# Five weight chunks ahead of U and V, block products in another order, and a last pair of heads with narrow matmuls in most slots

## The chip, the cores and the metric

One NeuronCore of one Trainium2 chip. The metric is device time in microseconds (us) of one execution, without the host; lower is better. Engines are named as in the profile: PE (matrix multiplies), PEld (its weight loads, which overlap), DVE, ACT, POOL, and SP, which issues the DMAs. Each engine takes its instructions in the order in which the program has them.

## What is computed

Three stages on a batch of 2 with 768 positions (reference, cut to what matters):

```python
# 1 attention: q, k, v [2, 8, 768, 64], masked by clusters of heads' queries and keys
mask = q_assign[:, :, :, None] == k_assign[:, :, None, :]
scores = np.where(mask, scale * np.matmul(q, k.transpose(0, 1, 3, 2)), -1e9)
attn = np.exp(scores - np.max(scores, axis=-1, keepdims=True))
x = np.matmul(attn / (np.sum(attn, axis=-1, keepdims=True) + 1e-09), v)   # -> [2, 768, 512]
# 2 mixer over positions and channels
theta = x @ w_theta
y = einsum(w_tok_r, x * np.cos(theta)) + einsum(w_tok_i, x * np.sin(theta))
u = x + y
x = u + np.maximum(u @ w_ch, 0.0)
# 3 low-rank mixer, then a wide layer: U [768, 32], V [32, 768], w_ch1 [512, 2048], w_ch2 [2048, 512]
u = x + (x.transpose(0, 2, 1) @ U @ V).transpose(0, 2, 1)
out = u + np.maximum(u @ w_ch1, 0.0) @ w_ch2
```

## The kernel before

x is kept transposed, as eight tiles `xT` of 128 channels by 768 positions (four of them, t = 0 to 3, per batch b; `hf` is a half of 384 positions). The program is written out by hand in the order in which each engine runs it, so an instruction waits for every earlier one on its engine as well as for its own inputs. PE has eight PSUM banks in a ring. Products in near-fp32 precision are made of three passes, with each factor split in a high and a low part: `wh`, `xh`, `uh`, `gh` and `wl`, `xl`, `ul`, `gl`.

**Weights** arrive as 64-bit words and are converted on the chip, one chunk (`Convert`) after the other in the order of a queue: ACT L385 (`magnitude`), then three DVE operations, L389 (`bits`), L393 (`top`), L397 (`low`), then ACT L402 makes `wh` and POOL L406 `wl`. A chunk is 128x768, or 128x512 where it is one of w_ch1. Each call of `conv_step()` that the program makes at fixed places issues the next DVE operation of the front chunk, and behind the last of them the two splits when the next step comes; `conv_until(dst, i)` steps on until a chunk is there. Three staging buffers hold loaded chunks. U and V are chunks too: from U the ACT L615 makes four block-diagonal tiles `ub` in 16 copies, from V ACT L621 and DVE L626 make `vs`. `weigh_pair(k)` takes two chunks of w_ch1 together and makes the sums of blocks of which the last stage's products are formed (ACT L465 and L478, POOL L466 to L480).

**Attention** goes by eight pairs of heads, g = 0 to 7, each in six slots p. A slot makes scores (`st`, PE L303, full 128-column matmuls) for which ACT L308 takes the exponentials `p`; from those come `pv` (L316) and the sums `l` (L335), in matmuls of 32 columns, "narrow" below. A unit of `next_pv` is eight narrow matmuls in the trace's count. Before, units stand only in the slots of `BURST = (2, 5)`, six in each, and `sum_keys` (24 narrow `l`) beside them; `max_rows` (L281 to L284) in slot 2 makes the row maxima `mrow`, which ACT L284 copies into `qp` for the second half of the pair's scores. `fill` issues what stands in the list `bg`, or conversion steps, up to a budget per slot. In the last pair (g = 7, `not nxt`) `bg` gets the splits of four finished tiles, `split_x` (ACT L510 `xh`, POOL L512 `xl`), at a cost of 0, so that all of them go in one call of `fill`.

**Mixer and low rank.** Theta and the position mixing (L525 to L574) are followed by `chmix(b, e)` (L585, L590: the product with w_ch; four per batch). `turn` (DVE L601) transposes finished tiles into `xt`. `low1(b)` is x@U, 24 matmuls of `xt` with `ub` (L636, 48 in the trace's count), `low2` the product with `vs`. The program has chmix(0, 0 to 3), each with `conv_step(3)` or `conv_step(2)`, then steps until U and V are there, chmix(1, 0), low1(0), chmix(1, 1), low2, chmix(1, 2 and 3).

**The wide layer, plain part:** four blocks f of w_ch1 by three pieces c of the positions. `ff1(c, f)` (L708) gives `g`, ACT L713 and DVE L715 split it into `gh` and `gl` (three buffers each), and `ff2(c, f)` (L727) adds its product with w_ch2 into four accumulators, two blocks behind (`AHEAD`). w2 chunk 1 covers rows up to f = 2, chunk 2 is first needed by ff2(0, 3). Beside them run DVE sums of halves (`u_sum`, L676) and their splits (`split_sum`, ACT L682, POOL L683: `u0t`, `u1t`).

**The wide layer, block products:** for k = 2 to 7 and both batches a `Quartet` makes four quarter results from seven products (`step`, six matmuls of L754 each) with DVE sums (L762), and `keep` turns each result into `g` by two ACT operations (L766, L767) and POOL L768. Its eight units (`unit`, six matmuls of L806 each) stand between the steps of the next quartet; unit 0 needs `g[1, 0]` and `g[0, 0]`. The temporaries of the sums (`temp`) take turns in the buffers of `gh` and `gl`. Between the steps of the first quartet stand the last two ff2, behind its steps 1 and 3.

```python
conv_load.extend(ff[:6])            # chunks ahead of U and V
conv_load.append(Convert(u_in, S, 0, [lambda c, g=g: keep_u(c, g) for g in range(4)], 32, 4))
conv_load.append(Convert(v_in, S, 0, [keep_v, keep_vl], 32))
conv_load.extend(ff[6:])
```

Before, the queue behind the three chunks of w_ch is (w1 is w_ch1, w2 is w_ch2): w1 0, w1 1, w2 0, w1 2, w1 3, w2 1, U, V, w2 2, then the pairs of w1 for the block products with a chunk of w2 now and then.

Of the kernel before, what the change touches and what calls it, by code (L numbers as in the profile page):

```python
# [41 lines left out]
def tile_cluster_block(ctx: ExitStack, tc: tile.TileContext, qk, v, cent, wth, wr, wi, wch,  # L42
                       u_in, v_in, w1, w2, cst, out):
    nc = tc.nc
# [408 lines left out]
    w1_t, w1p_t, lower = {}, {}, {}  # L453
# [242 lines left out]
    GF = 4  # L696
# [45 lines left out]
    class Quartet:  # L742
# [26 lines left out]
            self.g[i, hf] = t  # L769

        def step(self, n):
            x, y = (("11", "11"), ("12", "21"), ("s2", "t2"), ("s3", "t3"), ("s1", "t1"), ("22", "t4"), ("s4", "22"))[n]
            ps = bank("q")
            self.products(ps, x, y)
            if n == 0:
                self.u1 = self.temp(0)
                nc.scalar.activation(out=self.u1, in_=ps[:, :HALF], func=AF.Copy)
            elif n == 1:
                r = self.temp(1)
                self.add(r, ps, self.u1)  # L780
                self.keep(0, 0, r)
            elif n == 2:
                self.add(self.u1, ps, self.u1)
            elif n == 3:
                self.u2 = self.temp(0)
                self.add(self.u2, ps, self.u1)
            elif n == 4:
                r = self.temp(1)
                self.add(r, ps, self.u2)
                self.add(self.u1, ps, self.u1)  # L790
                self.keep(1, 1, r)
            elif n == 5:
                self.add(self.u2, ps, self.u2)
                self.keep(1, 0, self.u2)
            else:
                self.add(self.u1, ps, self.u1)
                self.keep(0, 1, self.u1)
# [41 lines left out]
    def attention():  # L839


        ORDER = [(0, 0), (0, 2), (0, 4), (1, 0), (1, 2), (1, 4)]
        BURST = (2, 5)
        pvq = deque()
        held[0] = True

        def next_pv():
            g, kt, hf = pvq.popleft()
            pv(g, kt, hf)
            if kt == NT - 1 and hf:  # L850
                pv_out(g)

        for g in range(NG):
            nxt = g + 1 < NG
            if nxt:
                load_v(g + 1)
            if g + 2 < NG:
                bg.extend(split_items(g + 2, nc.gpsimd))
                bg.extend(assign.pop(g + 2))
            if g + 3 < NG:  # L860
                for i in range(2):
                    load_raw(g + 3, i)
            if g == 1:
                conv_load.extend(weigh_in(wth, NP * DM, wth_t))
                conv_start()
            if g == 2:
                tok = [c for p in zip(weigh_in(wr, NT * S, wr_t), weigh_in(wi, NT * S, wi_t)) for c in p]
                conv_load.extend(tok[:6])
                conv_start()
                late = tok[6:]  # L870
            if g == 6:
                conv_load.extend(late)
                conv_start()
            if not nxt:
                for t in range(NP):
                    bg.append((0, lambda t=t: split_x(0, t, nc.gpsimd)))
            order = [(1, 0), None, (1, 2), None, (1, 4), None] if g == 0 else ORDER
            for p in range(NT):
                ready = len(pvq)
                if order[p]:  # L880
                    h, a = order[p]
                    scores_pair(g, h, a)
                    if h:
                        pvq.extend((g, kt, hf) for kt in (a, a + 1) for hf in range(2))
                if g == 0 and p < 2:
                    mask_direct(1, p, nc.scalar if p else nc.vector)
                if nxt:
                    max_pair(g + 1, p // 3, 2 * p % 6)
                    if p % 3 == 2:
                        max_join(g + 1, p // 3)  # L890

                while conv_after:
                    conv_after.popleft()()
                if p == 3 and g + 2 < NG:
                    mask_rows(g + 2)
                if g > 0 and p == 5:
                    bg.appendleft((.95, lambda: norm_x(g - 1)))
                    bg.appendleft((.97, lambda: spread(g - 1)))
                fill(2. if not nxt else 4.8 if p in BURST else .3)
                if p in BURST:  # L900
                    if p == 2 and g > 0:
                        max_rows(g, 1)
                        sum_keys(g - 1, 1)
                    if p == 5:
                        if nxt:
                            max_rows(g + 1, 0)
                        sum_keys(g, 0)
                    for _ in range(min(ready, 6)):
                        next_pv()
                    if p == 5 and g + 3 < NG:  # L910
                        (_, sims), *assign[g + 3] = assign_items(g + 3)
                        sims()
                if g > 0 and p == 2:
                    row_sums(g - 1)
            while bg:
                fill(.5)
        held[0] = False
        while len(pvq) > 1:
            next_pv()
        nc.scalar.activation(out=warm, in_=warm, func=AF.Sin)  # L920
        next_pv()
        sum_keys(NG - 1, 1)
# [95 lines left out]
    def mixer():  # L1018
# [5 lines left out]
        for n in range(len(seq) + LEAD):  # L1024
# [21 lines left out]
            if n == 11:  # L1046
                conv_load.extend(weigh_in(wch, NP * DM, wch_t))
                c2 = weigh_in(w2, NF * DM, w2_t)
                ff = []
                for k in range(NQ):  # L1050
                    if k == 1:
                        later = ff.pop()
                    if k < GF // 2:
                        ff.extend(Convert(w1, NF * DM, 2 * k + j, keep_split(w1p_t), width=DM) for j in range(2))
                    else:
                        ff.extend(weigh_pair(k))
                    if k == 1:
                        ff.append(later)
                    while c2 and c2[0].c0 < (k + 1) * 2 * DM:
                        ff.append(c2.pop(0))  # L1060
                conv_load.extend(ff[:6])
                conv_load.append(Convert(u_in, S, 0, [lambda c, g=g: keep_u(c, g) for g in range(4)], 32, 4))
                conv_load.append(Convert(v_in, S, 0, [keep_v, keep_vl], 32))
                conv_load.extend(ff[6:])
                conv_start()
            if 20 <= n <= 23:
                clear_u(n - 20)
# [29 lines left out]
        for n, w in enumerate(fs):  # L1097
            ff1(*w)
            if n == 0:
                low1(1)  # L1100
            if n in (1, 2):
                low2(1, 2 * n - 2)
                low2(1, 2 * n - 1)
# [12 lines left out]
        for k in range(GF // 2, NQ):  # L1116
            for b in range(2):
                q = Quartet(k, b)
                for n in range(7):
                    q.step(n)  # L1120
                    if was:
                        was.unit(n)
                    elif n in (1, 3):
                        ff2(*fs[(n - 1) // 2 - AHEAD])
                    if 0 < n < 6:
                        conv_step()
                if was:
# [62 lines left out]
```

## Time and profile before

| what | value |
|---|---|
| median of 3 runs | 697.5 us (696.27 to 698.05) |
| the profiled execution | 697.62 us |
| its span, from the first to the last instruction | 695.8 us |
| mean granted clock of PE, of full speed | 0.99 |
| PE busy | 672.8 us (97%) |
| DVE, ACT, POOL busy | 508.6, 348.4, 280.4 us |

The profile is that of one execution, whose span lies inside its time. Times in its rows are from the span's start. A row gives the start, the time from the first start to the last end of a group of like instructions, the engine, the line, what is written from what, and how many; in square brackets stand the idle time of the engine before it and what ended it. Matmuls overlap each other, so a stretch of PE is read from start to start.

### The profile page before, as it was taken

To read this page: it belongs to the slowest core of one execution; us is meant where nothing else is said; L and a number is where in the kernel's file an instruction comes from. 1 tells how busy PE (TensorE), PEld (TensorE's weight loads), DVE (VectorE), ACT (ScalarE), POOL (GpSimd) and SP (SyncE) were. 2 spreads that over 40 slices of the span, in tenths; PEclk is the share of its full clock that TensorE was granted. 3 is DMA by queue.
4 is the path that set the end of the run, shared out by engine and by line. 5 is a ranking of instruction groups with operands and counts; after the bars stand their busy time and mean duration, and the time that the engine had idled before them with its cause. 6 is when DMAs were issued, how large, how long until landed. Compare 5 with 4: busy or idle time off the path is not lost.

```text
span 695.8 us, 11957 instructions
## 1 busy us (share of the span) xinstructions
PE 672.8 (97%) x4563; PEld 576.0 (83%) x4564; DVE 508.6 (73%) x879; ACT 348.4 (50%) x713; POOL 280.4 (40%) x277
## 2 busy tenths in 40 slices
PE   8899999999998999999999969999989999999997
PEld 3567766756755599999999969898889999999997
DVE  6887898898997474468583957679487877877554
ACT  7657657656758444554555152334344444444221
POOL 8422313323227331114244112248655766656321
PEclk9899999999999999999999989999999999999999
DMA  6769788567423210002121130012213122210013
GB/s 208 196 144 264 196 192 243 159 165 190 141 91 106 77 31 3 1 24 85 57 71 24 58 106 1 0 31 75 78 34 90 62 60 90 61 32 1 0 40 143
DMA packets 21833, 63.15 MB, mean 91 GB/s; under 512 B 4272, under 2 KB 7216, under 8 KB 21776
## 3 DMA queue, kind: packets, MB, share of 16 engines
q1 hardware_dynamic: 21776, 62.39, 31.5%
q8 instruction: 36, 0.59, 0.3%
q14 instruction: 21, 0.17, 0.1%
HBM read 40.94 MB, written 3.15 MB: 63 GB/s over the span
## 4 chain that ended last, share of the span: by engine, by line
PE 82%; DVE 6%; ACT 5%; POOL 3%; issue 2%; DMA 2%; SPq 0%; POOLq 0%; DVEq 0%; ACTq 0%
PE y L567 14%; PE acc L806 14%; PE q L754 11%; PE pv L316 9%; PE st L303 7%; PE g L708 5%; PE th L525 5%; PE l L335 4%; PE acc L727 4%; PE smax L251 3%; PE h L585 2%; ACT p L308 2%; DVE mx L255 2%; PE h L636 2%; DMA st<-in_wth_dram 1%
## 5 line engine op out<-in xcount | busy, mean ns | idle before, releaser
L406 POOL TENSOR_TENSOR wl<-cv,wh 128x768 fp32r<-128x768 f32 (+1 forms) x33 | 60.6, 1838 | 109.8 <-ACT wh L402 92.6
L255 DVE TENSOR_REDUCE mx<-smax 128x1 f32<-128x512 f32 x144 | 89.6, 682 | 15.9 <-PE smax L251 15.9
L806 PE MATMUL acc<-g,wh 128*128 128x384 f32 x384 | 98.1, 335 | 2.9 <-POOL g L768 1.8
L308 ACT ACTIVATE p<-st 128x512 f32<-128x512 f32 x192 | 78.9, 513 | 43.2 <-PE st L303 42.2
L567 PE MATMUL y<-wh,z 128*128 128x384 f32 x384 | 87.6, 340 | 0.3 <-ACT z L545 0.3
L768 POOL TENSOR_TENSOR g<-sum,g 128x384 fp32r<-128x384 f32 x48 | 53.7, 1121 | 81.6 <-ACT g L767 74.2
L762 DVE TENSOR_TENSOR xT<-acc,xT 128x384 f32<-128x384 f32 x96 | 53.1, 555 | 37.4 <-PE acc L806 37.0
L303 PE MATMUL st<-qp,kp 128*128 128x256 f32 (+1 forms) x384 | 78.7, 349 | 0.3 <-ACT qp L284 0.2
L303 PEld LDWEIGHTS st<-qp,kp 128*128 128x128 f32 x384 | 58.7, 192 | 17.3 <-issue 5.3
L806 PEld LDWEIGHTS acc<-g,wh 128*128 128x128 f32 x384 | 69.3, 188 | 3.8 <-POOL g L768 2.4
L567 PEld LDWEIGHTS y<-wh,z 128*128 128x128 f32 x384 | 66.9, 188 | 0.5 <-ACT z L545 0.5
L766 ACT ACTIVATE sum<-sum 128x384 f32<-128x384 f32 x48 | 25.1, 524 | 81.7 <-DVE sum L762 81.7
L316 PE MATMUL pv<-p,v 128*32 128x384 f32 x768 | 65.5, 486 | 0.0
L806 PE MATMUL acc<-g,wl 128*128 128x384 f32 x192 | 64.1, 334 | 0.0
L762 DVE TENSOR_TENSOR sum<-q,sum 128x384 f32<-128x384 f32 x84 | 45.4, 552 | 19.3 <-PE q L754 16.9
L551 POOL TENSOR_TENSOR z<-tht,z 128x256 fp32r<-128x256 f32 x24 | 20.0, 834 | 92.9 <-ACT z L545 92.8
L316 PEld LDWEIGHTS pv<-p,v 128*32 128x32 f32 x768 | 31.6, 110 | 30.1 <-issue 21.6
L393 DVE SCALAR_TENSOR_TENSOR cv<-st,cv 128x768 int32<-128x768 int32 (+2 forms) x47 | 50.3, 1071 | 0.7
L397 DVE SCALAR_TENSOR_TENSOR cv<-st,cv 128x768 int32<-128x768 int32 (+2 forms) x47 | 48.8, 1038 | 0.5
L567 PE MATMUL y<-wl,z 128*128 128x384 f32 x192 | 48.8, 335 | 0.0
L251 PE MATMUL smax<-kp,qp 128*128 128x512 f32 x192 | 44.0, 348 | 3.0 <-ACT qp L177 1.9
L251 PEld LDWEIGHTS smax<-kp,qp 128*128 128x128 f32 x192 | 32.9, 191 | 12.7 <-issue 2.9
(171 smaller groups left out, 1508.8 us busy)
## 6 DMA issues: line engine op xcount, KB each, us to landing
st<-in_w_dram SPq DMA_DIRECT2D x17, 512.0 KB, 3.6
st<-in_w_dram SPq DMA_DIRECT2D x10, 768.0 KB, 4.2
raw<-in_qk_dram SPq DMA_DIRECT2D x16, 384.0 KB, 4.9
qp<-hi SPq DMA_DIRECT2D x26, 192.0 KB, 2.9
st<-in_wr_dram SPq DMA_DIRECT2D x6, 768.0 KB, 4.4
st<-in_wi_dram SPq DMA_DIRECT2D x6, 768.0 KB, 4.4
kp<-hi SPq DMA_DIRECT2D x32, 96.0 KB, 3.0
qp<-lo SPq DMA_DIRECT2D x32, 96.0 KB, 2.7
```

What stands on the lines that cost most here:

```text
L251: nc.tensor.matmul(out=ps[:, c:c + w], lhsT=qp[s, h, 0][:, (a + j) * P:(a + j + 1) * P], rhs=kp[s, h, 0][:, k0:k0 + w], start=True, stop=True)
L255: nc.vector.tensor_reduce(mx_t[g, h][:, o:o + n], ps.rearrange("p (n w) -> p n w", n=n), axis=AX.X, op=ALU.max)
L303: nc.tensor.matmul(out=ps[:, c:c + n], lhsT=kp[s, h, w][:, (a + j) * P:(a + j + 1) * P], rhs=qp[s, h, w][:, q0:q0 + n], start=(w == 0), st ...
L308: nc.scalar.activation(out=pt[g, h, a + j][:, q0:q0 + n], in_=ps[:, c:c + n], func=AF.Exp, scale=float(D) ** -0.5)
L316: nc.tensor.matmul(out=pvt[g][hf][r:r + 32, :HALF], lhsT=v_t[g][:, kt, r:r + 32], rhs=pt[g, r // 64, kt][:, cols(hf)], start=(kt == 0), st ...
L393: nc.vector.scalar_tensor_tensor(t, self.hw, SIGN, t, op0=ALU.bitwise_and, op1=ALU.bitwise_or)
L406: nc.gpsimd.tensor_tensor(t[:, :c.w], c.t, f32(c.hi[:, :c.w]), op=ALU.subtract)
L567: nc.tensor.matmul(out=yps[u, j][hf][:, :HALF], lhsT=lhs, rhs=w[st][e][:, hf * HALF:(hf + 1) * HALF], start=(st == 0 and n == 0), stop=(st ...
L754: nc.tensor.matmul(out=ps[:, :HALF], lhsT=w[a][:, j * P:(j + 1) * P], rhs=u_block(self.b, y, e, j), start=(n == 0), stop=(n == 5))
L762: nc.vector.tensor_tensor(out, ps[:, :HALF], x, op=ALU.add)
L768: nc.gpsimd.tensor_tensor(t[:, 1], r, f32(t[:, 0]), op=ALU.subtract)
L806: nc.tensor.matmul(out=ps[:, :HALF], lhsT=wv[a], rhs=self.g[i, hf][:, x], start=(m == 0), stop=(m == 5))
```

## The change

Three things are edited. First, in the last pair of heads the splits cost 1 in `bg`, `sum_keys(6, 1)` goes from slot 2 to slot 0, `sum_keys(7, 0)` stays in slot 5, and the units of `pv` stand as 2, 2, 2, 0, 4, 4 in the six slots instead of 6 in each of two. Second, the queue of weights becomes w1 0, w1 1, w2 0, w2 1, w1 2, U, V, w1 3, w2 2 and so on: U and V stand behind five chunks instead of six. A `conv_until` for w1 3 is written behind low1(1). Third, steps 4 and 5 of a quartet change places, with their additions, so that `g[1, 0]` comes from step 4 and `g[1, 1]` from step 5; and the last two ff2 stand behind steps 4 and 6 of the first quartet.

```diff
@@ Quartet.step
-            x, y = (("11", "11"), ("12", "21"), ("s2", "t2"), ("s3", "t3"), ("s1", "t1"), ("22", "t4"), ("s4", "22"))[n]
+            x, y = (("11", "11"), ("12", "21"), ("s2", "t2"), ("s3", "t3"), ("22", "t4"), ("s1", "t1"), ("s4", "22"))[n]
...
             elif n == 4:
                 r = self.temp(1)
                 self.add(r, ps, self.u2)
-                self.add(self.u1, ps, self.u1)
-                self.keep(1, 1, r)
+                self.keep(1, 0, r)
             elif n == 5:
                 self.add(self.u2, ps, self.u2)
-                self.keep(1, 0, self.u2)
+                self.add(self.u1, ps, self.u1)
+                self.keep(1, 1, self.u2)
@@ attention
             if not nxt:
                 for t in range(NP):
-                    bg.append((0, lambda t=t: split_x(0, t, nc.gpsimd)))
+                    bg.append((1., lambda t=t: split_x(0, t, nc.gpsimd)))
...
                 fill(2. if not nxt else 4.8 if p in BURST else .3)
-                if p in BURST:
+                if not nxt:
+                    if p == 0:
+                        sum_keys(g - 1, 1)
+                    if p == 2:
+                        max_rows(g, 1)
+                    if p == 5:
+                        sum_keys(g, 0)
+                    for _ in range(min(ready, (2, 2, 2, 0, 4, 4)[p])):
+                        next_pv()
+                elif p in BURST:
                     if p == 2 and g > 0:
                         max_rows(g, 1)
                         sum_keys(g - 1, 1)
                     if p == 5:
-                        if nxt:
-                            max_rows(g + 1, 0)
+                        max_rows(g + 1, 0)
                         sum_keys(g, 0)
@@ mixer, the queue of weights
                 for k in range(NQ):
-                    if k == 1:
-                        later = ff.pop()
                     if k < GF // 2:
                         ff.extend(Convert(w1, NF * DM, 2 * k + j, keep_split(w1p_t), width=DM) for j in range(2))
                     else:
                         ff.extend(weigh_pair(k))
-                    if k == 1:
-                        ff.append(later)
                     while c2 and c2[0].c0 < (k + 1) * 2 * DM:
                         ff.append(c2.pop(0))
-                conv_load.extend(ff[:6])
+                conv_load.extend(ff[:5])
...
-                conv_load.extend(ff[6:])
+                conv_load.extend(ff[5:])
@@ mixer, the plain part
             if n == 0:
                 low1(1)
+                conv_until(w1p_t, GF - 1)
@@ mixer, the first quartet
-                    elif n in (1, 3):
-                        ff2(*fs[(n - 1) // 2 - AHEAD])
+                    elif n in (4, 6):
+                        ff2(*fs[n // 2 - 2 - AHEAD])
```

PE in the last pair of heads, a piece of the difference at slot 1 (`st` the scores, `pv` a narrow product):

```order
 L303 MATMUL st<-qp_93,kp_95 128x512
 L303 MATMUL st<-qp_94,kp_96 128x512
+L316 MATMUL pv<-p_2582,v_2165 32x384 x2
+L316 MATMUL pv<-p_2754,v_2165 32x384 x2
+L316 MATMUL pv<-p_2582,v_2165 32x384 x2
+L316 MATMUL pv<-p_2754,v_2165 32x384 x2
 L303 MATMUL st<-qp_93,kp_95 128x512
 L303 MATMUL st<-qp_94,kp_96 128x512
```

Two units of narrow matmuls now stand between the scores of slot 1 and those of slot 2, where the scores followed each other.

ACT ahead of low1 (`wh` the high part of a chunk, `xh` that of x; of the rows `cv`, a chunk's first step, the one of 32x768 is V's and the last one ahead of it is U's). Before:

```order
L510 ACTIVATE xh_4633<-xT_2981 128x768
L402 ACTIVATE wh<-cv 128x512
L385 ACTIVATE cv<-st 128x768
L510 ACTIVATE xh_4684<-xT_3130 128x768
L402 ACTIVATE wh<-cv 128x512
L385 ACTIVATE cv<-st 128x768
L402 ACTIVATE wh<-cv 128x768
L385 ACTIVATE cv<-st 32x768
L615 ACTIVATE ub_4348<-cv 32x6x32
```

and of the change:

```order
L510 ACTIVATE xh_4633<-xT_2967 128x768
L402 ACTIVATE wh<-cv 128x768
L385 ACTIVATE cv<-st 128x768
L510 ACTIVATE xh_4684<-xT_3120 128x768
L402 ACTIVATE wh<-cv 128x512
L385 ACTIVATE cv<-st 32x768
L615 ACTIVATE ub_4351<-cv 32x6x32
```

One chunk fewer, with its three DVE operations, stands ahead of the copies of U into `ub`.

POOL in the plain part, a piece of the difference at the splits `u0t` (`L466` and `L467` belong to the first pair of w1, the added `wl` to w2 chunk 2, whose `wh` now stands on ACT right behind the `gh` of ff1(1, 1)):

```order
+L683 TENSOR_TENSOR u0t_5230<-t_5169,u0t_5229 128x768
+L406 TENSOR_TENSOR wl<-cv,wh 128x768
+L683 TENSOR_TENSOR u0t_5281<-t_5172,u0t_5280 128x768
+L683 TENSOR_TENSOR u0t_5341<-t_5218,u0t_5340 128x768
+L466 TENSOR_TENSOR w_5395<-cv,w_5395 128x256
 L467 TENSOR_TENSOR cv<-cv 128x256
```

The split of w2 chunk 2 came ahead of all of these before, and now stands between the first two.

## Rows read from the trace of the kernel before

**Rows 1.** The page, busy time and share of the span by engine.

```profile
PE 672.8 (97%) x4563; PEld 576.0 (83%) x4564; DVE 508.6 (73%) x879; ACT 348.4 (50%) x713; POOL 280.4 (40%) x277
```

**Rows 2.** The waits of PE: what waited for what, us, times, longest.

```profile
PE h L636 <- ACT ub L615: 6.2, 1, 6.2
PE mrow L281 <- ACT p L308: 2.1, 1, 2.1
...
PE acc L806 <- POOL g L768: 1.8, 2, 1.2
...
PE acc L806 <- ACT g L767: 1.1, 1, 1.1
```

**Rows 3.** Timeline of PE in the last pair of heads.

```profile
216.06 0.34 PE L281 MATMUL mrow<-identb,m 128*2 128x128 bf16 x6 [2.14 <-ACT p L308]
216.60 2.14 PE L335 MATMUL l<-p,ones 128*32 128x384 f32 x24 [0.21 <-ACT p L308]
218.56 4.05 PE L316 MATMUL pv<-p,v 128*32 128x384 f32 x48
222.55 4.45 PE L303 MATMUL st<-qp,kp 128*128 128x512 f32 x24
226.93 2.14 PE L335 MATMUL l<-p,ones 128*32 128x384 f32 x24
228.89 7.92 PE L316 MATMUL pv<-p,v 128*32 128x384 f32 x96
236.63 2.12 PE L335 MATMUL l<-p,ones 128*32 128x384 f32 x24
```

**Rows 4.** Timeline of ACT in the last pair of heads.

```profile
212.46 3.06 ACT L510 ACTIVATE xh<-xT 128x768 fp32r<-128x768 f32 x4
...
220.77 0.96 ACT L284 ACTIVATE qp<-mrow 2x384 fp32r<-2x384 f32 x2
```

**Rows 5.** Timeline of PE one pair earlier: scores between wide matmuls.

```profile
187.47 1.56 PE L303 MATMUL st<-qp,kp 128*128 128x512 f32 x8
188.87 0.85 PE L251 MATMUL smax<-kp,qp 128*128 128x512 f32 x4
```

**Rows 6.** Timeline of DVE ahead of low1(0), last steps of two chunks.

```profile
393.01 0.96 DVE L397 SCALAR_TENSOR_TENSOR cv<-st,cv 128x768 int32<-128x768 int32 x1
...
400.22 0.92 DVE L397 SCALAR_TENSOR_TENSOR cv<-st,cv 128x768 int32<-128x768 int32 x1
```

**Rows 7.** Timeline of ACT there, twelve of the sixteen copies of U.

```profile
401.17 3.38 ACT L615 ACTIVATE ub<-cv 32x192 f32<-32x192 f32 x12 [5.46 <-DVE cv L397]
```

**Rows 8.** Timeline of PE, the two low1 (b = 0 and b = 1).

```profile
405.90 7.42 PE L636 MATMUL h<-xt,ub 128*128 128x128 f32 x48 [6.22 <-ACT ub L615]
...
430.36 5.52 PE L636 MATMUL h<-xt,ub 128*128 128x128 f32 x48
```

**Rows 9.** Windows of 2 us: PE, PEld, DVE, ACT, POOL busy, PEclk, DMA share, GB/s.

```profile
214.00:216.00 2.00, 0.00 (x0) 0.00 (x0) 0.00 (x0) 2.00 (x5) 2.00 (x2) 1.00 0.83 230
...
402.00:404.00 2.00, 0.00 (x0) 0.00 (x0) 1.52 (x2) 1.98 (x9) 0.00 (x0) 0.71 0.82 236
...
408.00:410.00 2.00, 2.00 (x12) 2.00 (x12) 1.97 (x4) 1.48 (x3) 0.00 (x0) 0.58 0.00 0
```

**Rows 10.** Timeline at ff2(0, 3), its first matmul on PE, then ACT.

```profile
459.39 0.40 PE L727 MATMUL acc<-gh,wh 128*128 128x512 f32 x1
...
460.15 0.41 ACT L465 ACTIVATE w<-cv 128x256 fp32r<-128x256 f32 x1
```

**Rows 11.** Timeline of ACT, then of POOL: the splits of chunks 768 wide.

```profile
483.68 0.85 ACT L402 ACTIVATE wh<-cv 128x768 fp32r<-128x768 f32 x1 [0.97 <-DVE cv L397]
...
484.67 2.30 POOL L406 TENSOR_TENSOR wl<-cv,wh 128x768 fp32r<-128x768 f32 x1 [1.90 <-ACT wh L402]
...
395.05 1.84 POOL L406 TENSOR_TENSOR wl<-cv,wh 128x768 fp32r<-128x768 f32 x1 [5.39 <-ACT wh L402]
```

**Rows 12.** A window of the block products, columns as in rows 9.

```profile
515.00:600.00 85.00, 85.00 (x493) 85.00 (x492) 66.20 (x109) 37.17 (x67) 54.03 (x45) 1.00 0.23 69
```

## The prediction, made before the changed kernel ran

> **What bounds the kernel now.** I read the page's shares first: PE is busy 672.8 of the span's 695.8 us [rows 1], so only some 23 us of idle PE can go, and an instruction taken off another engine is worth what PE stops waiting. So next I read the list of PE's waits [rows 2]: one of 6.2 us stands out, low1(0) waiting for `ub`, then 2.1 us in the last pair of heads and 2.9 us (1.8 and 1.1) among the block products. The rest of the list lies where the change moves nothing. Then the timelines at those three places. Last the windows, for what an idle PE does to its clock: in the 6.2 us wait the granted clock falls from 2.4 to 1.2 GHz (0.71 as a mean of 402 to 404 us, so at about 402.8; 0.58 over 408 to 410, so back at about 409.7), while the idle 214 to 216 us kept 1.00 [rows 9].
>
> The sum is made on the profiled execution, 697.62 us: its span of 695.8 and 1.8 around it, which nothing here touches. It is 0.12 above the median of the three runs, so the forecast stands for the median as well.
>
> **The last pair of heads.** PE waits 2.14 us before `mrow` and 0.21 before `l` [rows 3] because ACT makes four `xh` in a row, 3.06 us, ahead of the exponentials that it needs [rows 4]. Spread over two calls of `fill`, only two `xh` stand ahead of the exponentials of slot 1 (1.53 us less), and the narrow work behind slots 0 and 1 needs exponentials of the pair before alone. The wait should go: −2.35 us. Two costs come instead. Slot 3's scores need `qp`, which ACT now copies behind the other two `xh` and the exponentials of slot 2: I put its end at 220.5 by the time scale of before, where `qp` began at 220.77 [rows 4], against 220.1 for PE's arrival, +0.35. And narrow and wide matmuls now alternate more often: narrow blocks stand behind slots 0, 1, 2, 4 and 5, where they stood behind 2 and 5, so three more pairs of switches. Their price is in the rows. 96 `pv` from 228.89 to 236.63 take 7.74, so 48 take 3.87; 48 with scores behind them take 3.99 (218.56 to 222.55), 0.12 more [rows 3]. Eight scores behind wide ones take 1.40 (187.47 to 188.87), so 24 take 4.20 [rows 5]; between two narrow blocks they took 4.38 (222.55 to 226.93) [rows 3], 0.18 more. So 0.30 for a pair, +0.9 for three. Sum: −2.35 + 0.35 + 0.9 = **−1.1**; bounds −2.35 (both costs hidden) and 0. The conversion steps that no longer fit into this pair, some four, are made up early in the mixer's steps, on engines that wait for PE there.
>
> The page "TensorEngine Tiling (Array Packing)" of the Trainium skill, section Key Properties, speaks against this part: changing the tiling mode drains TensorE. It gives no price; the 0.30 agrees with a drain in sign, and by the pure count of matmuls, without that rule, the term would be −2.0 and the time 687.7.
>
> **U and V behind five chunks.** PE is free for low1(0) 6.22 us ahead of 405.90 [rows 8], at 399.68. What it waits for is U: its last DVE step was at 400.22 [rows 6], and the first twelve copies into `ub` ran from 401.17 [rows 7]; the last four followed when PE had begun. In the new order U stands in the place of w2 chunk 1, whose last DVE step ended at 393.97 [rows 6]. So `ub` begins at about 394.0; 3.38 for twelve copies [rows 7], a third of that for four more, and under 0.9 for the L385 between them (estimated from the 0.85 of a 768-wide ACT operation [rows 11]) end at about 399.2 to 399.4. The last transposes of xT into `xt` then end at about 399.5, as V's 32-row steps lie between. All this is ready just when PE is: **−6.22**, with a margin of 0.2 to 0.5 only. The clock goes with the wait: low1(0) took 7.42 where low1(1), the same 48 matmuls, took 5.52 [rows 8], **−1.90**. Bounds: 0 for the clock if over half the wait stays, and I keep a late U of up to 3 as a rival. Moving the chunks costs nothing by itself: each is converted once as before. `conv_until` behind low1(1) does nothing, as w1 3 has been converted while the program stepped on for V and later.
>
> **The price: w2 chunk 2.** It was converted before the plain part, and now three steps later, so its last DVE operation falls between ff1's fourth and fifth, and its two splits behind the sixth ff1: ACT makes `wh` right behind `gh` where L465 stood (460.15), POOL makes `wl` behind `u0t`. ff2(0, 3) needs both at once; PE came to it at 459.39 [rows 10]. `wh` takes 0.85 [rows 11] from 460.15, to 461.0, so PE stands idle for about 1.6. Two passes use `wh` (0.23 each, start to start), the third wants `wl`: 1.84 to 2.30 us on POOL [rows 11] from 461.0, to 463.0 or so, and PE idles about 1.5 again. All later passes follow at once. **+3.1**; bounds 0 (the two splits run earlier than I place them) and 3.4 (the 2.30 row). The work behind ff2 on DVE and POOL, the sums of halves, comes with several us in hand before the first quartet wants it.
>
> **Block products.** With `g[1, 0]` made one step earlier, unit 0 no longer waits for it; and two ff2, twelve matmuls each, no longer push the first steps apart but stand between the later steps and the units that need them. PE's waits for `g`, 1.1 for ACT's half and 1.8 for POOL's in two pieces of which one is 1.2 [rows 2], so 0.6 the other, lose their cause: **−2.9**. The DVE sum of step 3 now waits for ff2(2, 2) to give its buffer free, and behind it on DVE wait the sums of step 4; PE finds free banks for two more steps and goes on. From the second quartet on every conversion comes three steps later than before. PE was without an idle moment for 85 us there [rows 12], and the weights that I followed are ready some 8 us before their products, so I cost that at nothing. Bounds of the part: −2.9, and 0, as such waits can come up again at other places.
>
> **Sum:** −1.1 − 6.22 − 1.90 + 3.1 − 2.9 = −9.0, so 697.62 − 9.0 = **688.6 us**, 1.3% less.
>
> **The rivals.**
> - **The clock falls at w2 chunk 2.** Two idle stretches of 1.5 us with 0.46 of matmuls between them are nearly 3.5 us of little work; 6.2 us of idle lowered the clock for some 6.9 us, 2.14 us of idle did not [rows 3, 9]. If it falls, ff1 and ff2 behind it run at half speed for up to 6.9 us and lose 3.4: 692.0. The page "TensorE: Matmul & The Clock Gate" of the Trainium skill, section on HAM oscillation, names idle gaps between bursts of matmuls as what throttles TensorE; the trace agrees for the 6.2 us, and no run here shows a gap like this one. 0.2.
> - **The new wait does not come.** `wh` and `wl` of chunk 2 are made while ff1 runs, since nothing in the way of DVE stands there: 688.6 − 3.1 = 685.5. Against it: the splits are issued by a later conversion step, and that stands behind `gh` on ACT. 0.1.
> - **U stays late.** The margin of 0.2 to 0.5 is thin: if V's steps or a slower DVE make `xt` or `ub` late by 1 to 3 us, and the clock falls at the longer of these, 1 to 5 of the 8.1 are lost: 689.6 to 693.6. 0.12.
> - **The last pair gives nothing.** Waits for `qp` and more switching eat the 2.35: 689.7. Inside the range, 0.08.
> - **Slower: the lag of conversions starves the quartets.** Three steps later for every pair of chunks; if each of the five later pairs of quartets waits for `w1` sums or `g` as long as the first did, 2.9 us, that is +14.5, to 703.1. It decides from 1.8 us per pair on, as 9.0 / 5. Against it: DVE is busy 66.2 of 85 us and POOL 54.0 [rows 12], so both have room. 0.03.
> - **The change does not do what it says:** narrow matmuls in most slots are only moved, and the written `conv_until` is idle, so those two change nothing by themselves; that is in the sum already.
>
> **How the numbers follow.** 0.47 for the forecast. The range goes from the rival without the new wait, with 1.0 of the last pair's 1.25 in costs hidden as well, 684.5, to the fallen clock with 1.5 of a late U beside it, 693.5; it leaves out starvation, the worst of a late U, and mishaps that I don't see, 0.15 to 0.2 in all. A measurement of this kernel tells a difference of 0.3%, 2.1 us, from none. Faster by more than that needs under 695.4: all cases but starvation and a very late U together with a fallen clock, 0.93; same 0.04; slower 0.03.
>
> **What would show it.** The list of PE's waits should have lost `ub`, `mrow` and both `g`, and have a new one, for `wh` (L402) and `wl` (L406), about 1.5 each, at ff2(0, 3). low1(0) should take about 5.5, and the clock be 1.00 from the prologue on. PE in the last pair should show five narrow blocks. Wrong would be: an idle of over 1 us before low1(0); a clock under 1.00 behind ff2(0, 3); waits of L754 for `wh` (L478) in the quartets; or a theta stage that begins less than 0.5 us earlier than before.

## The result, and the profile after

The changed kernel took 687.41 us (median of 4 runs, 686.36 to 689.28) where the kernel before took 696.88 (695.95 to 698.05): ratio 0.9866, 95% interval 0.9838 to 0.9894. The forecast was 688.6, the range 684.5 to 693.5. Its profiled execution took 686.36 us. The line of the cores and the page's busy time answer to [rows 1]:

```profile
core 0: 684.2 us, clock 0.995
```

```profile
PE 669.6 (98%) x4564; PEld 573.8 (84%) x4564; DVE 513.2 (75%) x879; ACT 347.7 (51%) x713; POOL 281.0 (41%) x277
```

The list of PE's waits answers to [rows 2]. `ub`, `mrow` for `p`, and `g` are gone; `wh` and `wl` are new, and the first line was there before:

```profile
PE smax L251 <- ACT qp L177: 1.9, 2, 1.2
PE acc L727 <- ACT wh L402: 1.5, 1, 1.5
PE acc L727 <- POOL wl L406: 1.3, 1, 1.3
```

Where the time went is seen best on PE itself, cut at the first matmul of each part. The table gives the lengths in us, from the starts in the timeline of PE.

| stretch of PE | before | after | difference | forecast |
|---|---|---|---|---|
| to the first scores of the last pair | 209.45 | 208.05 | −1.40 | 0 |
| last pair of heads, to theta (L525) | 29.22 | 27.66 | −1.56 | −1.1 |
| theta and position mixing, to chmix (L585) | 140.03 | 140.04 | 0.01 | 0 |
| chmix, low1(0), low2, to the first ff1 (L708) | 48.89 | 40.68 | −8.21 | −8.12 |
| plain part, to the first block product (L754) | 68.08 | 71.31 | +3.23 | +3.1 |
| block products, to the last L806 | 196.32 | 192.59 | −3.73 | −2.9 |

The first line is not the change's: no edit reaches there, and over the runs below this stretch was anything from 207.2 to 209.5. It goes with the clock: it took 207.2 to 207.5 in the six profiled executions whose granted clock was at its lower level for 3.4 us within the first 28 us, and 207.7 to 209.5 in the seven where that lasted 6.8 us, these two among them. Without that line the span got 10.3 us shorter, and the time 9.9, as 2.2 us now lie outside the span and 1.8 did before.

The timeline of PE in the last pair answers to [rows 3]:

```profile
208.05 1.68 PE L303 MATMUL st<-qp,kp 128*128 128x512 f32 x8
209.66 2.14 PE L335 MATMUL l<-p,ones 128*32 128x384 f32 x24
211.62 1.47 PE L316 MATMUL pv<-p,v 128*32 128x384 f32 x16
213.02 1.66 PE L303 MATMUL st<-qp,kp 128*128 128x512 f32 x8
214.61 1.50 PE L316 MATMUL pv<-p,v 128*32 128x384 f32 x16
216.03 1.68 PE L303 MATMUL st<-qp,kp 128*128 128x512 f32 x8
...
219.21 3.08 PE L303 MATMUL st<-qp,kp 128*128 128x512 f32 x16
222.21 2.79 PE L316 MATMUL pv<-p,v 128*32 128x384 f32 x32
224.93 1.68 PE L303 MATMUL st<-qp,kp 128*128 128x512 f32 x8
```

No bracket stands in it, nor in the lines left out: neither the wait for `p` nor the forecast one for `qp` (at 219.21) is there. Each start of scores behind a narrow block is about 1.6 us ahead of the next narrow block, where eight scores took 1.40 between wide matmuls [rows 5]. On ACT, answering to [rows 4], the `xh` now come in twos, and `qp` behind the second two:

```profile
211.06 1.59 ACT L510 ACTIVATE xh<-xT 128x768 fp32r<-128x768 f32 x2
...
215.34 1.60 ACT L510 ACTIVATE xh<-xT 128x768 fp32r<-128x768 f32 x2
...
218.31 0.95 ACT L284 ACTIVATE qp<-mrow 2x384 fp32r<-2x384 f32 x2
```

Ahead of low1(0), in the timelines of ACT, DVE and PE in turn (answering to [rows 6 to 8]), the last copies into `ub`, the last transposes, and the two low1:

```profile
395.14 1.11 ACT L615 ACTIVATE ub<-cv 32x192 f32<-32x192 f32 x4
...
395.26 1.14 DVE L601 STREAM_TRANSPOSE xt<-xT 128x192 f32<-128x192 f32 x4
...
396.55 5.52 PE L636 MATMUL h<-xt,ub 128*128 128x128 f32 x48
...
419.19 5.52 PE L636 MATMUL h<-xt,ub 128*128 128x128 f32 x48
```

`ub` is complete at 396.25 and `xt` at 396.40, PE starts at 396.55 without idle: the margin is 0.15 to 0.3 us. Both low1 now take 5.52.

At ff2(0, 3), in the timelines of PE, ACT and POOL, answering to [rows 10]:

```profile
449.86 0.50 PE L727 MATMUL acc<-gh,wh 128*128 128x512 f32 x1 [1.48 <-ACT wh L402]
450.20 0.40 PE L727 MATMUL acc<-gl,wh 128*128 128x512 f32 x1
451.86 0.50 PE L727 MATMUL acc<-gh,wl 128*128 128x512 f32 x1 [1.27 <-POOL wl L406]
...
448.98 0.83 ACT L402 ACTIVATE wh<-cv 128x768 fp32r<-128x768 f32 x1
...
449.89 1.92 POOL L406 TENSOR_TENSOR wl<-cv,wh 128x768 fp32r<-128x768 f32 x1 [3.08 <-ACT wh L402]
```

The two splits stand where the order put them, and PE waits for one after the other.

In the block products, unit 0 of the first quartet on PE, which waited twice before, at 511.32 and 513.01 (those rows stand further down):

```profile
501.62 0.52 PE L806 MATMUL acc<-g,wh 128*128 128x384 f32 x2
501.97 0.33 PE L806 MATMUL acc<-g,wl 128*128 128x384 f32 x1
502.15 0.51 PE L806 MATMUL acc<-g,wh 128*128 128x384 f32 x2
```

### The profile page after: what moved, and what is told of

Its sections match the earlier page's. It is cut to its first block, busy times and chain, and to the rows that moved or that the text cites. A ratio compares the mean times of both kernels' runs of the same rounds, so it can differ in the third digit from the quotient of the medians.

```text
span 684.2 us, 11966 instructions
## 1 busy us (share of the span) xinstructions
PE 669.6 (98%) x4564; PEld 573.8 (84%) x4564; DVE 513.2 (75%) x879; ACT 347.7 (51%) x713; POOL 281.0 (41%) x277
## 4 chain that ended last, share of the span: by engine, by line
PE 85%; ACT 5%; DMA 3%; DVE 3%; issue 2%; SPq 1%; POOL 1%; POOLq 0%
PE y L567 15%; PE acc L806 15%; PE q L754 13%; PE pv L316 8%; PE st L303 7%; PE h L585 5%; PE th L525 5%; PE g L708 4%; PE acc L727 4%; PE l L335 4%; PE smax L251 3%; ACT p L308 2%; DVE mx L255 2%; PE h L636 2%; DMA st<-in_wth_dram 1%
## 5 line engine op out<-in xcount | busy, mean ns | idle before, releaser
L406 POOL TENSOR_TENSOR wl<-cv,wh 128x768 fp32r<-128x768 f32 (+1 forms) x33 | 58.5, 1774 | 113.8 <-ACT wh L402 96.6
L806 PE MATMUL acc<-g,wh 128*128 128x384 f32 x384 | 97.5, 334 | 0.0
L806 PEld LDWEIGHTS acc<-g,wh 128*128 128x128 f32 x384 | 69.4, 188 | 0.0
L806 PE MATMUL acc<-g,wl 128*128 128x384 f32 x192 | 64.1, 334 | 0.0
L393 DVE SCALAR_TENSOR_TENSOR cv<-st,cv 128x768 int32<-128x768 int32 (+2 forms) x47 | 53.0, 1128 | 0.6
L397 DVE SCALAR_TENSOR_TENSOR cv<-st,cv 128x768 int32<-128x768 int32 (+2 forms) x47 | 53.1, 1130 | 0.4
```

The costliest lines, as they stand in the source:

```text
L397: nc.vector.scalar_tensor_tensor(t, self.lw, 29, t, op0=ALU.logical_shift_right, op1=ALU.bitwise_or)
L406: nc.gpsimd.tensor_tensor(t[:, :c.w], c.t, f32(c.hi[:, :c.w]), op=ALU.subtract)
L806: nc.tensor.matmul(out=ps[:, :HALF], lhsT=wv[a], rhs=self.g[i, hf][:, x], start=(m == 0), stop=(m == 5))
```

## The experiments

The theory is that the edits act on separate places, add up, and each works by the wait named in the prediction. The rivals are named in each expectation. Stretches are those of the table. Each variant ran beside the kernel before on one chip, but the variants are spread over three chips. So they are compared by the stretches of their profiles: from theta on, and in the pair, those that an edit should leave alone agree within 0.15 us, but for the clock, which is told where it differs.

### One part undone at a time

**The last pair as before.** Cost 0, and the slots of `BURST` for g = 7 too:

```diff
-                    bg.append((1., lambda t=t: split_x(0, t, nc.gpsimd)))
+                    bg.append((0, lambda t=t: split_x(0, t, nc.gpsimd)))
...
-                if not nxt:
-                    if p == 0:
-                        sum_keys(g - 1, 1)
...
+                if p in BURST:
...
```

> The changed kernel with the last pair of heads as before: splits of x at cost 0, narrow matmuls in slots 2 and 5, six units each. If the three parts of the change add up, the wait of 2.1 us for mrow comes back, the narrow blocks are two again, and the time is that of the changed kernel + 1.6 us (the stretch from the pair's first scores to theta was 29.2 us before and 27.7 after); the waits for wh and wl at ff2(0, 3) stay at 1.5 and 1.3. Rival: the four conversion steps that the pair lost are what delays w2 chunk 2; then those two waits go as well and the time is 1.6 lower than the changed kernel instead of higher.

Measured: 690.16 us (686.99 to 691.51), ratio to before 0.9906 (0.9874 to 0.9939). In its profile the pair takes 29.22 again, with waits of 2.14 and 0.21 for `p`, and every other stretch is that of the changed kernel within 0.03; the waits for `wh` and `wl` stay at 1.48 and 1.27. By time this execution, 686.99, is the shortest of its four; the others, 689.16 to 691.51, have a granted clock of 0.990 to 0.993 where it has 0.996, and are not profiled. So the median stands 2.75 above the changed kernel's, where 1.6 was expected, and that part of it is open. By the profile the pair's part is 1.56, and the conversion steps that the pair lost have nothing to do with w2 chunk 2.

**The queue as before.** `ff[:6]`, `ff[6:]`, w1 3 put back ahead of the chunk of w2, no `conv_until`:

```diff
...
-                conv_load.extend(ff[:5])
+                conv_load.extend(ff[:6])
...
-                conv_load.extend(ff[5:])
+                conv_load.extend(ff[6:])
...
```

> The changed kernel with the queue of weights as before, six chunks ahead of U and V. If the parts add up, the 6.2 us wait for ub and the low clock in low1(0) come back (+8.2) and the waits at ff2(0, 3) go (-3.2): + 5.0 us, with no wait of L806 for g. Rival: the waits for g in the block products went because every conversion comes three steps later, not by the order of the steps; then they come back too, 2.9 to 3.7 more, and the time is + 8 to 9 us.

Measured: 691.75 us (691.00 to 692.97), ratio 0.9937 (0.9916 to 0.9959). The wait for `ub` is back at 6.22, chmix to ff1 takes 49.65, the plain part 68.08 and the block products 192.60, without a wait for `g`. So the waits for `g` did not go because conversions come later. The 0.76 by which the stretch from chmix to ff1 is longer than before comes of the clock: its record shows the lower level from 401.8 to 408.7 us, and PE went on at 403.28, so 5.4 us of work lay in it where 3.8 did before (405.90 to 409.7).

**The quartets as before.** Old order of steps 4 and 5, and the two ff2 behind steps 1 and 3:

```diff
-            x, y = (("11", "11"), ("12", "21"), ("s2", "t2"), ("s3", "t3"), ("22", "t4"), ("s1", "t1"), ("s4", "22"))[n]
+            x, y = (("11", "11"), ("12", "21"), ("s2", "t2"), ("s3", "t3"), ("s1", "t1"), ("22", "t4"), ("s4", "22"))[n]
...
-                    elif n in (4, 6):
-                        ff2(*fs[n // 2 - 2 - AHEAD])
+                    elif n in (1, 3):
+                        ff2(*fs[(n - 1) // 2 - AHEAD])
```

> The changed kernel with the quartet's steps in the old order and the last two ff2 behind steps 1 and 3. If the parts add up, L806 waits for g three times again, 2.9 us in all and 3.7 from first to last matmul of the block products: + 3.7 us against the changed kernel. Rival, that the later conversions took these waits away: 0.

Measured: 690.55 us (690.34 to 690.96), ratio 0.9920 (0.9899 to 0.9940). The block products take 196.30, +3.71, with four waits for `g`:

```profile
PE acc L806 <- POOL g L768: 2.3, 4, 0.7
```

They stand at other places than before, as the conversions do. And a thing that no edit of this run touches: its plain part takes 72.90, 1.59 more than the changed kernel's. Its windows of 2 us behind the wait for `wl`, columns as in [rows 9]:

```profile
450.00:452.00 2.00, 0.89 (x3) 0.69 (x4) 1.83 (x2) 0.00 (x0) 2.00 (x2) 0.83 0.65 270
452.00:454.00 2.00, 2.00 (x6) 1.63 (x5) 1.17 (x2) 0.00 (x0) 1.30 (x1) 0.50 0.00 0
454.00:456.00 2.00, 2.00 (x12) 1.73 (x12) 1.33 (x2) 0.00 (x0) 0.00 (x0) 0.82 0.00 0
```

The granted clock was at its lower level, 1.2 GHz, from about 451.3 to 454.7. That is the forecast's rival of the clock. In the profiled execution of the changed kernel it did not happen, at the same waits; the count over all profiled executions is below.

### The new wait

**Conversion steps from the second ff1 on.**

```diff
-            if n > 2:
+            if n > 0:
                 conv_step(1 + n % 2)
```

> The changed kernel with conversion steps in the plain part from its second ff1 on instead of its fourth (three steps more, ahead of the fourth). If the waits at ff2(0, 3) come from w2 chunk 2 being three steps late, both go, and the time is 3.2 us lower than the changed kernel. Rival: DVE, which carries low2 and the splits of u there, is then late for ff1 of the second piece, and 1 to 3 us come back at L708 as waits for uh or ul: 0 to -2.

Measured: 684.97 us (684.15 to 685.65), ratio 0.9838 (0.9819 to 0.9856). Both waits at ff2(0, 3) are gone; the plain part takes 69.96, so 1.35 less than in the changed kernel and 1.88 more than before. The rival is right in kind: DVE is late, though not for L708 but for `gl`. Timelines of PE, DVE and POOL:

```profile
432.50 0.40 PE L727 MATMUL acc<-gh,wl 128*128 128x512 f32 x1
434.44 0.51 PE L727 MATMUL acc<-gh,wh 128*128 128x512 f32 x1 [1.54 <-DVE gl L715]
...
431.30 2.48 DVE L393 SCALAR_TENSOR_TENSOR cv<-st,cv 128x768 int32<-128x768 int32 x1
433.71 0.68 DVE L715 SCALAR_TENSOR_TENSOR gl<-g,gh 128x512 fp32r<-128x512 f32 x1
...
430.81 2.16 POOL L664 TENSOR_TENSOR ul<-xT,uh 128x768 fp32r<-128x768 f32 x1 [17.11 <-ACT uh L663]
```

L393, which takes 0.96 by itself, took 2.48 beside POOL's split, and `gl` stood behind it. The page "SBUF — State Buffer" of the Trainium skill, section "SBUF: two separate sides", says that DVE, in an operation with two SBUF inputs as this one, and GpSimd share a port pair which the first holds for its whole instruction. By that rule DVE would begin at POOL's end, 432.97, and end at 433.9. It ended at 433.78, so the trace agrees within 0.15 us.

**The three steps ahead of low1(1).** DVE stands idle there in the changed kernel. First its row, then the steps of this run in that place:

```profile
425.89 0.41 DVE L645 CAST h1s<-h 32x512 fp32r<-32x512 f32 x1 [5.18 <-ACT h L642]
...
420.28 0.55 DVE L389 TENSOR_SCALAR cv<-cv 128x768 int32<-128x768 int32 x1
420.86 0.96 DVE L393 SCALAR_TENSOR_TENSOR cv<-st,cv 128x768 int32<-128x768 int32 x1
421.86 0.96 DVE L397 SCALAR_TENSOR_TENSOR cv<-st,cv 128x768 int32<-128x768 int32 x1
425.54 0.42 DVE L645 CAST h1s<-h 32x512 fp32r<-32x512 f32 x1 [2.73 <-ACT h L642]
```

The edit:

```diff
             if n == 0:
-                low1(1)
                 conv_until(w1p_t, GF - 1)
+                conv_step(3)
+                low1(1)
```

> The changed kernel with the three DVE steps of w2 chunk 2 ahead of low1(1), where DVE has nothing to do for 5 us while it waits for low1(1). If lateness of that chunk is the whole cause of the two waits at ff2(0, 3), and the wait for gl that the steps at the second ff1 brought came from their place alone, the plain part takes 68.1 us from its first ff1 to the first block product (71.3 changed, 70.0 with the earlier steps): 3.2 us less than the changed kernel, some 1.9 less than the run before with early steps. Rival, that the chunk's splits on ACT and POOL delay another thing there: between 69 and 71.

Measured: 682.93 us (682.79 to 683.15), ratio 0.9814 (0.9794 to 0.9834). The plain part takes 68.12, without a wait of PE, and every other stretch but the start is that of the changed kernel. So the place of three DVE operations of one chunk was the whole price of moving U and V ahead, and it need not be paid.

### The last pair

**Bursts kept, splits spread:** the slots of before, with the splits at cost 1.

```diff
-                if not nxt:
-                    if p == 0:
-                        sum_keys(g - 1, 1)
...
+                if p in BURST:
...
```

> The changed kernel with the narrow matmuls of the last pair in slots 2 and 5 as before, but the splits of x still at cost 1, two per slot. If the wait for mrow is made by the four xh ahead of the exponentials, two of them (1.5 us) less leave about 0.6 to 0.8 of it, and the pair takes 27.6 us (29.2 before, 27.7 changed). If it goes because narrow work in slots 0 and 1 gives ACT time, the wait stays over 1.5 and the pair takes 28.7 to 29.2.

One run: 687.27 us. The pair takes 27.78, with 0.68 and 0.21 of the waits left. The first theory holds: two `xh` out of the way take 1.46 off the wait. The narrow matmuls in most slots are worth 0.12 on top.

**Two narrow blocks.**

```diff
-                    for _ in range(min(ready, (2, 2, 2, 0, 4, 4)[p])):
+                    for _ in range(min(ready, (6, 0, 0, 0, 0, 8)[p])):
```

> The changed kernel with the last pair's units of pv as 6, 0, 0, 0, 0, 8 by slot: narrow blocks behind slots 0 and 5 alone, three fewer than in the changed kernel. If a pair of switches between wide and narrow costs 0.30 us, the pair takes 26.8 instead of 27.7, provided ACT keeps up with the scores that follow each other. Rival, that ACT's exponentials then hold PE up for banks: a wait for p of 0.5 to 1.5 comes back and the pair takes 27.3 to 28.5.

One run: 687.53 us, the pair 29.74. That is outside both of the expectation's cases: the wait that came is for `qp`, which neither names. Timelines of PE, then ACT:

```profile
217.99 0.51 PE L303 MATMUL st<-qp,kp 128*128 128x512 f32 x1
220.99 4.25 PE L303 MATMUL st<-qp,kp 128*128 128x512 f32 x23 [2.50 <-ACT qp L284]
...
218.50 1.65 ACT L308 ACTIVATE p<-st 128x512 f32<-128x512 f32 x4
219.99 0.96 ACT L284 ACTIVATE qp<-mrow 2x384 fp32r<-2x384 f32 x2
```

`qp` stands on ACT behind the exponentials of slot 2, and with no narrow work between `mrow` and slot 3 nothing covers it. This run doesn't give the price of the switches by itself.

**Splits at once, narrow matmuls as changed:** cost 0 in the changed kernel.

```diff
-                    bg.append((1., lambda t=t: split_x(0, t, nc.gpsimd)))
+                    bg.append((0, lambda t=t: split_x(0, t, nc.gpsimd)))
```

> The changed kernel with the four splits of the last pair at cost 0, all in slot 0, and narrow matmuls in most slots as changed. Narrow work in slots 0 and 1 moves PE's need for the second slot's exponentials by some 5 us, so if that by itself covers the 3.06 us of xh, no wait for p comes and the pair takes 27.7 us as in the changed kernel: then either half of the edit removes the wait. If the splits must be spread, 1 us or more of a wait stays and the pair takes 28.7 or more.

One run: 688.82 us, the pair 29.06. No wait for `p` comes at `mrow`, as the narrow work in slots 0 and 1 covers the four `xh`, but 1.14 us for `qp` does:

```profile
219.13 0.50 PE L303 MATMUL st<-qp,kp 128*128 128x512 f32 x1
220.78 2.84 PE L303 MATMUL st<-qp,kp 128*128 128x512 f32 x15 [1.14 <-ACT qp L284]
```

On ACT a `wh` (L402) and an L385 of conversion steps, which came later in the changed kernel, stand ahead of `qp`. So the narrow matmuls alone take away the wait that they were to take away, and lose nearly all of it to the switches and to the wait for `qp`: 0.16 is left (29.22 to 29.06). The spread splits alone bring 1.44 (29.22 to 27.78), and carry the gain.

### The block products

**Old order of the steps, ff2 as changed:**

```diff
-            x, y = (("11", "11"), ("12", "21"), ("s2", "t2"), ("s3", "t3"), ("22", "t4"), ("s1", "t1"), ("s4", "22"))[n]
+            x, y = (("11", "11"), ("12", "21"), ("s2", "t2"), ("s3", "t3"), ("s1", "t1"), ("22", "t4"), ("s4", "22"))[n]
...
```

> The changed kernel with steps 4 and 5 of the quartets in the old order; the two ff2 stay behind steps 4 and 6. If the order of the steps is what takes the waits for g away, L806 waits for g at the end of the first pair and once later, and the block products take 194.5 us or more (192.6 changed, 196.3 before). If the place of the two ff2 does it alone: 192.6.

One run: 690.1 us, block products 195.10, with three waits for `g`:

```profile
PE acc L806 <- POOL g L768: 1.6, 3, 0.7
```

**ff2 as before, new order of the steps:**

```diff
-                    elif n in (4, 6):
-                        ff2(*fs[n // 2 - 2 - AHEAD])
+                    elif n in (1, 3):
+                        ff2(*fs[(n - 1) // 2 - AHEAD])
```

> The changed kernel with the last two ff2 behind steps 1 and 3 of the first quartet as before; the steps stay in the new order. With the steps in the old order alone the block products took 195.1 us, with both undone 196.3, with neither 192.6. If the place of the ff2 and the order of the steps each take away waits of their own, this gives 193.8 (192.6 + 1.2). If the order alone is enough, 192.6.

One run: 689.37 us, block products 192.59, no wait for `g`. So the order of the steps alone removes every wait. The two ff2 behind steps 4 and 6 bring 1.2 with the old order (196.30 to 195.10) and nothing with the new one.

### The best of both

**One split per slot,** narrow matmuls in slots 2 and 5, steps ahead of low1(1):

```diff
-                    bg.append((1., lambda t=t: split_x(0, t, nc.gpsimd)))
+                    bg.append((2., lambda t=t: split_x(0, t, nc.gpsimd)))
...
-                fill(2. if not nxt else 4.8 if p in BURST else .3)
+                fill((2., 2., 2., 2., 4., 4.)[p] if not nxt else 4.8 if p in BURST else .3)
...
```

> The kernel with the steps ahead of low1(1), and in the last pair narrow matmuls in slots 2 and 5 as before, with the splits of x at cost 2, one per slot in slots 0 to 3, and conversion steps behind them. With two splits per slot 0.68 and 0.21 of the wait were left; one xh of 0.77 less ahead of the exponentials leaves none, and no switches are added: the pair takes 26.9 us, 0.7 less than the changed kernel's, and the time is 0.7 lower than with the steps ahead alone, 682.2. If the wait is held by another thing than the xh, the pair takes 27.7 and the time is 682.9. Rival on the other side: conversions that come later in the pair make the mixer wait for a chunk, 1 us or more there.

Measured: 681.79 us (681.63 to 682.32), ratio to before 0.9797 (0.9782 to 0.9813), the lowest of this study against the changed kernel's 0.9866. Its lead over the kernel with the steps ahead alone, 0.9814 (0.9794 to 0.9834), lies within the intervals; the profiles show it in the pair, 27.06 for 27.65. The mixing takes 140.12 for 140.04, so no chunk is late by the 1 us of the rival. The pair was expected at 26.9 with no wait; one of 0.20 is left:

```profile
212.15 2.14 PE L335 MATMUL l<-p,ones 128*32 128x384 f32 x24 [0.20 <-ACT p L308]
```

It also prices the switches: 27.06 with two narrow blocks and 0.20 of wait, 27.66 with five and none, so (27.66 − 26.86) / 3 = 0.27 us for a pair of switches. The idle time may be taken off as it is shown here: the pair with its waits of 2.14 and 0.21 took 29.22, which is 2.16 more for 2.15 more of idle.

## Why the prediction was right, step by step

**The bound.** That only PE's waits were to be had, and which three, held: everything gained stands in those stretches of PE.

**The last pair,** −1.1 forecast, −1.56 measured. The wait of 2.35 went and the switches cost what the rows said, 0.27 measured for 0.30. The step that failed is the +0.35 for `qp`: PE reaches the scores of slot 3 at 219.21 without a wait. The end of `qp` was forecast well: 219.26, or 220.66 on the time scale of before (the pair starts 1.40 earlier), where I had 220.5. PE's arrival was not: 219.21 is 220.61 on that scale, where I had 220.1. I had not put it later for the two pairs of switches that now lie ahead of it, which at 0.27 each make up the difference. And the first matmul of the slot doesn't wait for `qp`, as the two variants with a wait show; the second starts at 219.54, 0.28 behind the end of `qp`. So the wait was near, and it came, of 1.14 and 2.50, in those two variants. The extra switches took back 0.8 us, and the kernel without them is the faster in this stretch. The page "TensorEngine Tiling (Array Packing)" of the Trainium skill, section Key Properties, says that a change of the tiling mode drains TensorE; the trace agrees in sign with this price, for which the page has no figure.

**U and V,** −8.12 forecast, −8.21 measured: the wait of 6.22, 1.90 of clock, and the margin of 0.15 to 0.3 at the start of low1(0) where 0.2 to 0.5 stood in the text. One reading was wrong without effect on the sum: the last four copies into `ub` did not follow when PE had begun, but began at 405.49 behind an L385, and PE began at 405.90 behind the first of them.

**w2 chunk 2,** +3.1 forecast, +3.23 measured, at the place and by the two splits named. What I had as a rival with a chance of 0.2, the fall of the clock there, came in more executions than not: of the eight profiled executions that have both waits, five show the lower clock behind them and a plain part of 72.8 to 72.9, three (the changed kernel's, and those with the pair undone and with two narrow blocks) do not and have 71.3. The five profiled kernels without the pair of waits, the one before among them, never show it at that place. Its price is 1.6 us, about half the 3.4 that I gave, as the lower clock lasted 3.4 us there and not 6.9. That the changed kernel's profile has +3.23 and not +4.8 here is luck: it fell on the side without it. Its three other executions are 0.8 to 2.9 us longer, at granted clocks of 0.992 to 0.994 for 0.995. The fall would fit, and so would a longer start of the span; as they are not profiled, it is not shown which. Which executions get it, the runs don't settle.

**The block products,** −2.9 forecast, −3.73 measured: the term was mis-sized, and one of its two reasons was wrong. The size is in the rows of before, read from start to start (timeline of PE):

```profile
509.92 0.34 PE L806 MATMUL acc<-g,wl 128*128 128x384 f32 x1
511.32 0.44 PE L806 MATMUL acc<-g,wh 128*128 128x384 f32 x1 [1.07 <-ACT g L767]
513.01 0.44 PE L806 MATMUL acc<-g,wh 128*128 128x384 f32 x1 [1.24 <-POOL g L768]
513.29 0.34 PE L806 MATMUL acc<-g,wl 128*128 128x384 f32 x1
```

Such a matmul follows the one before it by 0.17 where nothing waits. From 509.92 to 511.32 are 1.40, so 1.23 lost where the bracket says 1.07; from there to 513.01 are 1.69, so 1.52 for 1.24; and the next start comes after 0.28, 0.11 more. Together with the later one of 0.60, at 607.48, which by the same reading cost 0.88, that is 3.74. I had added up the brackets. The reason that was wrong is the two ff2: with the steps in the new order their place changes nothing. The term that I had put at nothing, three steps of lag in the later quartets, held: no wait of L754 and none of L806 is in the profile.

**The sum and the rivals.** By the stretches the change was worth 10.3 us where 9.0 was forecast: 0.5 of the difference is the pair's, 0.8 that of the block products. The median, 687.41, came as near to 688.6 as it did with the help of things that no term holds, the start of the span (207.2 to 209.5) and what may be a fallen clock in the other executions. Of the rivals, the new wait came, U was not late, the quartets did not starve.

## What to carry to other kernels

When a queue of background work is reordered so that one item comes earlier, look up what now comes later by its length and who needs it first: here the gain of 8.2 us cost 3.2 at one chunk, and three operations put where their engine stood idle brought all of it back. Of an edit with two halves that aim at one wait, run each alone: the spread splits and the order of the steps did the work, and the narrow matmuls in most slots and the moved ff2 added 0.12 us and nothing. Price a wait of PE from start to start of its matmuls, not by the idle time in brackets.

## What the runs showed of the hardware that was not expected

- Between wide matmuls that overlap where nothing waits, a short wait of PE cost some 0.25 us more than the idle time shown: 0.27 on average for the three waits for `g` (3.73 for 2.91 in brackets), 0.24 for each of the two at ff2(0, 3) (3.23 for 2.75). In the last pair, where the wait stands between scores and `mrow` or narrow matmuls, it cost what is shown (2.16 for 2.15).
- Two idle stretches of 1.48 and 1.27 us with two matmuls between them were followed by a granted clock at the lower level, 1.2 GHz, in five of eight profiled executions, though 2.14 us in one piece was not in either that has it, nor 2.50 us in the one with two narrow blocks. The page "TensorE: Matmul & The Clock Gate" of the Trainium skill, section on HAM oscillation, speaks of idle gaps between bursts of matmuls as what throttles TensorE. These five agree with it in kind and the other three don't show it; that section has no case with gaps as short as these.
- The same wait of 6.22 us cost 8.21 in one kernel and, with the queue undone, 8.97 (49.65 for 40.68) in another, by where in the wait the clock fell: 3.0 us ahead of PE's return in the first, 1.5 us ahead in the second, and both times the lower level lasted 6.8 us.
